# A gated-GELU block in two-level Winograd form: unit 4 in an order of its own, its sums on GpSimd, and operands of the down stage asked for sooner

## The chip, the cores and the metric

The kernel runs on one core of a Trainium2 chip. A core has TensorE (PE in the profile, with its weight loads as PEld), VectorE (DVE), ScalarE (ACT), GpSimd (POOL) and SyncE (SP, here the queue that issues all transfers), an on-chip memory in 128 partitions (SBUF), eight accumulation banks (PSUM) and 16 DMA engines. The metric is the device time of one execution in microseconds; three executions before the change took 537.00, 539.53 and 540.08 us, median 539.53.

## The reference

```python
B, S, Dm, Df = 1, 2048, 1024, 3584          # bfloat16 inputs
g = jnp.einsum("bsd,df->bsf", x, w_gate)
u = jnp.einsum("bsd,df->bsf", x, w_up)
h = jax.nn.gelu(g, approximate=True) * u
return jnp.einsum("bsf,fd->bsd", h, w_down)
```

## The kernel before

**Passes and units.** The 2048 tokens are two passes `p` of 1024, each cut into two halves `c` of 512 (a bank holds 128 x 512 numbers). The 3584 hidden columns are 14 units `u` of 256. Gate and up of a unit are computed as a 2 x 2 block product (contraction halves, column halves, token halves) with seven products in place of eight, Winograd's form. The weight side needs sums `s1` to `s4` (four-chunk tiles of 128 x 512, for gate and up each), the token side differences `t1` to `t4` and a cast `tb`. A product of four chunks is four matmuls of 128 x 128 x 512.

**Units 0 to 3** run one pass at a time (`items`, `unit`). At the end of the last item GpSimd also makes what unit 4 needs.

**Units 4 to 13** (`JOINT = 4`) run both passes together, and three of the seven products are cut once more by the same form. `X` is s4 times tb, `H` is s3 times t3, `K` is the raw quarter times t4. Each becomes seven half products `X1` to `X7` of two matmuls (14 in place of 16). They need new sums: `split_b` or `split_b3` make `n1`, `n2`, `n4` and an in-place difference from the token side, once for all units; `split_sums` (through `half_sums`) makes four half-size tiles `q1` to `q4` from the weight side, in every unit. `H` is cut from unit `DIVIDED7` on; before that it runs whole (16 matmuls).

**What sets the order.** The order is written out by hand. `SEQUENCE` is a list of steps of one joint unit; each step is issued to its engine at its place, and every engine works through its own list in order. `P1pi`, `P6pi`, `P5pi`, `S`, `G`, `X`, `H`, `K` are matmuls; `p`, `u2`, `v`, `xz`, `kz`, `ky`, `y`, `f0`, `f1`, `e00`, `e10`, `e01`, `ha`, `ga`, `gb`, `hb`, `sg`, `sh` are ACT copies, casts and gelus; `c11a`, `x00`, `m11a` and their like are DVE additions and multiplications. A step with `-` belongs to the unit before. A step with `@` is a place for side work (`side_work`): sums on GpSimd for this and the next unit, loads, and the sums of the down weights. Four banks `E` and four banks `F` change places from unit to unit.

**Down weights.** The down product uses the same form with 14 chunks `j`. For each chunk, `fetch_wd` loads two tiles, `keep_whole` makes three difference tiles `m` on GpSimd, and `store_made` writes them to DRAM (`td`); `KEEPS` says in which unit. Chunks in `STAY` keep two of them in SBUF for the first down pass, the others are loaded back (`load12`).

**Down.** `down(0)` and `down(1)` follow: the raw products `e` (14 steps of four matmuls), the next 14 into `c`, then the products of sums. A step list (`agenda`, `tails`, `more_0`) places loads and DVE sums. The hidden tiles `h` are stored to DRAM (`hd`) by the units and loaded back by `load_h`. Their SBUF space holds token sums until the units no longer read them: `room` gives `tb` and three `n` the tile `h00`, `t2` and `t1` the tile `h10`, and so on. So a load of `h00` waits for the last `X` of unit 13.

**Slots.** Nearly every small tile is one of 59 slots of 2 KB per partition; a new tile waits until the last reader of the old one is done.

Of the kernel before, what the change touches and what calls it, by code (L numbers as in the profile page):

```python
# [10 lines left out]
def kernel(  # L11
# [33 lines left out]
    NU = NFB // 2  # L45
    NWARM = 7
    JOINT = 4
    DIVIDED7 = 5
    STAY = 4, 5, 6
    KEEPS = [(u, n) for u in range(5, 14) for n in range({7: 2, 9: 2, 11: 2, 13: 3}.get(u, 1))]  # L50
    H, Q, R2 = NJ // 2, N // 2, range(2)
    SLOTS = 59
    SEAM = 3
    LAG = 3
    BIG12 = (0, 2), (8, 10)
    AT12 = [0, 0, 2, 2, 5, 5, 9, 12, 16, 18, 22, 27, 29, 31], [4, 4, 8, 8, 12, 12, 15, 16, 18, 20, 22, 27, 29, 31]
    AT12S = [6, 7, 9, 10, 13, 14, 16, 18, 20, 28, 29, 30, 31, 33]
    EARLY = 8
    AT73 = [30 + 2 * j if j < 7 else 38 + j for j in range(NJ)]
# [32 lines left out]
    def pool(out, a, b, op):  # L92
        nc.gpsimd.tensor_tensor(out=out, in0=a, in1=b, op=op)  # L93
# [200 lines left out]
                got.append(t)  # L294
        return n

    def split_b3(part, eng=pool):
        n = ns.setdefault("t3", [[], [], [], []])
        for k in range(2):
            b11, b12, b21, b22 = [T[p]["t3"][h + k] for h in (0, 2) for p in range(2)]  # L300
            if part == k:
                n1, n2, n4 = [slot([P, N], f32r, "n") for _ in range(3)]
                eng(n1, b12, b11, SUB)
                eng(n2, b22, n1, SUB)
                eng(n4, b21, n2, SUB)
                for i, t in ((0, n1), (1, n2), (3, n4)):
                    n[i].append(t)
            if part == 2:
                eng(b12, b22, b12, SUB)
                n[2].append(b12)  # L310

    def half(ps, lhs, rhs, fresh=False):
# [1 line left out]
            matmul(ps, lhs[:, k], rhs[k], fresh and k == 0, k == 1)  # L314

    SEQUENCE = (
        "@start -a00u P100 -a10u P101 @tb.0 -a00z P111 -m22a p101 @tb.1 -a01u P110 p100 -v11+ "
        "-g21a P601 -a01z @keep p110 P600 -a11u -hb2 X1 u201 -m21a P610 u200 -m22b xz1 X5 -a10y "
        "P501 p111 -a10z @s3 u210 X6 -a11z @store P500 v01 -a11y xz6 S0 -g21b x6y X7 @t3.0 v00 "
        "-m21b P510 sg c11a xz7 X2 X4 v10 @t3.1 P611 x00 f0 x01 ha H1 @t4.0 X3 u211 x7y S1 ga x10 "  # L320
        "@s1 H5 e00 m12a P511 @free gb c11b y5 H6 m11a H2 v11 K1 @t4.1 e10 x11 G0 kz1 v00+ H7 f1 "
        "H3 m12b K6 @late e01 @s2 e11 G1 ha2 e10y kz6 H4 K5 v10+ sh K2 hb v01+ @s4 K7 ky5 K3 m11b "
        "K4 kz7 @end "
    ).split()

    def joint_ops(u, E, F):
# [137 lines left out]
    def keep_whole(j):  # L464
        ra, rb = wraw.pop(j)
        m = made[j] = [slot([P, N], f32r, "m") for _ in range(3)]
        pool(m[0], ra[:, N:], ra[:, :N], SUB)
        pool(m[1], rb[:, N:], m[0], SUB)
        pool(m[2], rb[:, :N], m[1], SUB)

    def store_made(j):
        if j in STAY:
            q12[j] = made[j][:2]
        for n, m in enumerate(made.pop(j)):
            nc.sync.dma_start(out=td[:, j, n], in_=m.bitcast(f32))

# [116 lines left out]
        at_tail(1, -1 if n < 11 else 2 * n - 20, fetch12, n)  # L593
    for j in range(NJ):
        for last in range(2):
            at_tail(last, AT12[last][j], lambda j, last=last: load12(j, BIG12[last]), j)
        at_tail(0, 49 + 0.65 * j, load4, j)
        at_tail(0, 54 + 0.55 * j, make_sa, j)
    for t in range(H):
# [295 lines left out]
    def at_p5(n):  # L895
        u, p = items[n]
        if n == 0:
            pool_behind(t["t4"][-1])
            new_s(2, "s1", "s2", "s3", "s4")
        elif n == 1:  # L900
            new_s(3, "s1", "s2", "s3", "s4")
        elif n == 2:
            T[1] = sums_t(1, pool, place1)
            T[1].make("t1", "t2", "t3", "t4")
        elif n == 3:
            new_s(0, "s1", "s2", "s3", "s4")
            ss.pop(2), ss.pop(3)
            new_s(2, "s1", "s2")
        elif n == 4:
            new_s(2, "s3", "s4", "sa")  # L910
            new_s(3, "s1", "s2")
        elif n == 5:
            new_s(3, "s3", "s4", "sa")
            new_s(JOINT, "s1", "s2")
        elif n == 6:
            new_s(JOINT, "s4")

    keeps = {}
    for j, (u, n) in zip([*range(4), *range(7, NJ), *STAY], KEEPS):
        keeps[u, n] = j  # L920

    def load_next(u):
# [11 lines left out]
    def side_work(u, what):  # L934
        def made(kind, n):
            if (u, n) in keeps:
                kind(keeps[u, n])

        more = u + 1 < NU
        name, part = what[:2], int(what[3:]) if what[2:3] == "." else None  # L940
        if what == "start":
            if u == JOINT:
                load_next(u + 1)
            made(fetch_wd, 1)
        elif what == "keep":
            made(keep_whole, 0)
            if u == JOINT:
                split_b3(0, dve)
                split_b3(1)
                ns["t4"] = split_b("t4", dve, place_n)  # L950
        elif what == "store":
            made(store_made, 0)
            made(fetch_wd, 2)
        elif what == "s3":
            new_s(u, "s3")
            if u == JOINT + 1:
                split_b3(2)
        elif name == "tb":
            if u > JOINT:
                half_sums(u, name, part)  # L960
        elif name == "t3":
            half_sums(u, "t4" if u == JOINT else name, part)
            if more and part == 1:
                made(keep_whole, 1)
        elif what == "t4.0" and not more:
            half_sums(u, name, 0)
            half_sums(u, name, 1)
        elif what == "t4.1" and not more:
            made(keep_whole, 1)
            made(keep_whole, 2)  # L970
        elif name == "t4" and u > JOINT:
            half_sums(u, name, part)
        elif name in ("s1", "s2", "s4"):
            if more:
                new_s(u + 1, what)
        elif what == "late":
            made(store_made, 1)
            if (u + 1, 0) in keeps:
                fetch_wd(keeps[u + 1, 0])
        elif what == "end":  # L980
            made(store_made, 2)
            load_next(u + 2)
        if not more:
            last_loads(what)
# [2 lines left out]
    loads = {(0, 0): [3], (1, 1): [0], (3, 0): [2], (5, 0): [JOINT]}  # L987

    def last_loads(what):
        for n in {"start": range(4), "store": range(4, 8), "t4.0": range(8, 11), "s1": range(11, NJ)}.get(what, ()):  # L990
            fetch12(n)
        if what == "free":
            new_h(0, 0)
            for j0, j1 in ((0, 2), (2, 6), (6, 10), (10, NJ)):
                load_h(0, 0, 0, j0, j1)
            new_h(1, 0)
            for j0, j1 in ((0, 4), (4, 8), (8, NJ - 2)):
                load_h(0, 1, 0, j0, j1)
        if what == "end":
            new_h(1, 1), new_h(0, 1)  # L1000
            for j0, j1 in ((0, 4), (4, 8)):
                load_h(0, 0, 1, j0, j1)
                load_h(0, 1, 1, j0, j1)
                load12(j0 // 2, BIG12[0])

    with tc.manual_schedule(engines={ENG.Activation}):
        for n, (u, p) in enumerate(items):
# [41 lines left out]
            def p4(c12):  # L1049
                times(p, 2 * u, 1, gelu(c12[0]), c12[1])  # L1050
                if first:
                    whole_p4(u, p, odd, ss[u], after_first, behind_p4)
                else:
                    if n == len(items) - 1:
                        more_room()
                        ns["tb"] = split_b("tb", pool, place_n)
                        half_sums(JOINT, "tb", 0), half_sums(JOINT, "tb", 1)
                    whole_p4(u, p, (Ea, Eb)[b], ss[u], ahead_of_p4, behind_p4)

            if first:  # L1060
                banks = odd, cc, dd
# [9 lines left out]
        last = None  # L1071
        for u in range(JOINT, NU):
            now = joint_ops(u, E, F)
            for name in SEQUENCE:
                if name[0] == "@":
                    side_work(u, name[1:])
                elif name[0] != "-":
                    now[name]()
                elif last:
                    last[name]()  # L1080
            last = now
            E, F = F, E
# [4 lines left out]
    def more_0(step):  # L1087
        if step == 0:
            load_h(0, 0, 1, 8, NJ)
            load_h(0, 1, 1, 8, NJ - 1)  # L1090
        if step in (56, 59, 61):
            kh, c = {56: (0, 0), 59: (1, 0), 61: (0, 1)}[step]
            new_h(kh, c)
            for j0, j1 in ((0, 4), (4, 8), (8, NJ)):
                load_h(1, kh, c, j0, j1)
        if step == 46:
            fetch_early(0), fetch_early(4)
        if step == 63:
            new_h(1, 1)
            for j0, j1 in ((0, 4), (4, 8), (8, NJ)):  # L1100
                load_h(1, 1, 1, j0, j1)
# [33 lines left out]
```

## Time and profile before

| what | value |
|---|---|
| three runs | 537.00, 539.53, 540.08 us |
| profiled execution, its own time | 536.89 us |
| its span on the chip | 535.1 us |
| mean granted TensorE clock | 0.997 |
| PE busy | 523.2 us (98%) |
| DVE, ACT, POOL busy | 398.1, 290.9, 338.0 us |
| first matmul of unit 4, of the first down pass | 108.8 us, 356.9 us |
| last matmul ends | 531.8 us |

The units and the two down passes follow each other, so the span is read by stages. The page gives each engine's busy time in 40 slices and by group of instructions; a matmul counts as busy from its start to a modelled end (about 0.4 us), while matmuls follow each other every 0.22 to 0.23 us, so gaps are read from starts. The trace lacks some matmul records: a lone step of 0.42 to 0.46 us between two starts is one missing record.

### The profile page before, as it was taken

Reading aid. Unit: us, or ns where it says so; the run is one execution under the profiler, and the core shown is the slowest. Engines: PE = TensorE matmul, PEld = TensorE weight load, DVE = VectorE, ACT = ScalarE, POOL = GpSimd, SP = SyncE. Lnnn points to the kernel's source line nnn. Section 1 sums busy time; section 2 is a strip of 40 time slices with the busy share of each in tenths; the row PEclk is TensorE's granted clock in tenths of the full one; section 3 lists DMA queues with packets and bytes.
Section 4 is the critical chain, followed back from the end, with each engine's and each line's share of the span. In section 5 each row is a group of like instructions: output and inputs, shape, how many; then the busy total and the mean of one; then the engine's idle time right before and its main releaser. Section 6 shows DMA issues by size and latency. Waiting matters only on the chain.

```text
span 535.1 us, 7968 instructions
## 1 busy us (share of the span) xinstructions
PE 523.2 (98%) x2362; PEld 369.9 (69%) x2393; DVE 398.1 (74%) x597; ACT 290.9 (54%) x533; POOL 338.0 (63%) x344
## 2 busy tenths in 40 slices
PE   9999999997999999999999999989999999999997
PEld 5568686865676766767666776754688885488887
DVE  2984646599779898898979888894889335868934
ACT  3545655554687867878786877852125501132430
POOL 1169999999999989999999999940000000000394
PEclk9999999998999999999999999999999999999999
DMA  9687641330526274554727273899987999993642
GB/s 245 140 205 154 133 119 50 108 108 21 165 101 217 79 226 153 164 157 154 255 78 253 85 240 121 291 331 405 400 301 215 389 367 384 392 319 113 220 129 69
DMA packets 106538, 107.75 MB, mean 201 GB/s; under 512 B 19712, under 2 KB 84864, under 8 KB 106496
## 3 DMA queue, kind: packets, MB, share of 16 engines
q1 hardware_dynamic: 106496, 107.25, 62.6%
q8 instruction: 19, 0.31, 0.3%
q14 instruction: 23, 0.19, 0.1%
HBM read 74.58 MB, written 29.49 MB: 194 GB/s over the span
## 4 chain that ended last, share of the span: by engine, by line
PE 90%; SPq 4%; DVE 3%; DMA 2%; issue 1%; ACT 0%; DVEq 0%; ACTq 0%
PE bank L111 90%; SPq L779 2%; DVE h L90 2%; DMA h<-hd 1%; DVE n L90 1%; SPq L785 1%; DMA x<-in_x_dram 0%; SPq L132 0%; DVE w L90 0%; SPq L765 0%; DVE st L90 0%; DVE p L90 0%; DVE xz L90 0%; ACT bank L335 0%; ACT p L344 0%
## 5 line engine op out<-in xcount | busy, mean ns | idle before, releaser
L111 PE MATMUL bank<-h,s 128*128 128x512 f32 x472 | 129.6, 401 | 4.6 <-ACT u L107 3.5
L93 POOL TENSOR_TENSOR q<-q 128x256 fp32r<-128x256 f32 x28 | 24.3, 900 | 149.7 <-PE bank L111 149.2
L111 PE MATMUL bank<-xT,w 128*128 128x512 bf16 (+1 forms) x448 | 107.8, 376 | 1.3
L111 PEld LDWEIGHTS bank<-h,s 128*128 128x128 f32 x472 | 88.8, 188 | 26.4 <-ACT u L107 4.0
L93 POOL TENSOR_TENSOR s<-w 128x512 fp32r<-128x512 bf16 (+1 forms) x82 | 87.2, 1084 | 13.1 <-DMA w<-in_w_gate_dram 11.7
L111 PEld LDWEIGHTS <-w 128*128 128x128 bf16 x504 | 45.0, 98 | 59.4 <-issue 14.1
L111 PE MATMUL bank<-t,s 128*128 128x512 f32 x276 | 74.6, 402 | 0.0
L107 ACT COPY p<-bank 128x512 f32<-128x512 f32 x76 | 42.7, 590 | 34.7 <-PE bank L111 29.1
L111 PE MATMUL bank<-q 128*128 128x512 f32 x248 | 61.5, 390 | 0.0
L111 PEld LDWEIGHTS bank<-t,s 128*128 128x128 f32 x276 | 52.4, 190 | 12.1
L90 DVE TENSOR_TENSOR q<-h,h 128x512 fp32r<-128x512 bf16 x56 | 38.3, 685 | 21.3 <-DMA h<-hd 21.3
L111 PEld LDWEIGHTS bank<-q 128*128 128x128 f32 x248 | 46.5, 188 | 9.8
L107 ACT COPY u<-bank 128x512 f32<-128x512 f32 x62 | 35.9, 592 | 24.5 <-PE bank L111 23.2
L93 POOL TENSOR_TENSOR s<-s,s 128x256 fp32r<-128x256 f32 x57 | 43.3, 786 | 1.9 <-PE bank L111 0.2
L93 POOL TENSOR_TENSOR s<-s,w 128x512 fp32r<-128x512 f32 (+1 forms) x40 | 41.2, 1047 | 1.7 <-PE bank L111 0.5
L93 POOL TENSOR_TENSOR s<-w,s 128x512 fp32r<-128x512 bf16 (+1 forms) x40 | 41.5, 1054 | 0.0
L111 PEld LDWEIGHTS <-h 128*128 128x128 bf16 x224 | 21.7, 98 | 28.3 <-DMA h<-hd 2.3
L90 DVE TENSOR_TENSOR xz<-bank,xz 128x512 f32<-128x512 f32 x40 | 27.5, 690 | 15.9 <-PE bank L111 7.4
L111 PE MATMUL bank<-raw,h 128*128 128x512 bf16 x156 | 34.7, 379 | 1.6 <-DMA h<-hd 1.4
L93 POOL TENSOR_TENSOR m<-raw,m 128x512 fp32r<-128x512 bf16 x28 | 34.6, 1234 | 2.2
L102 ACT CAST tb<-raw 128x512 fp32r<-128x512 bf16 x28 | 17.0, 632 | 33.4 <-DMA raw<-in_w_down_dram 14.6
L90 DVE TENSOR_TENSOR h<-g,bank 128x512 bf16<-128x512 f32 x42 | 28.6, 684 | 6.4 <-ACT g L205 3.5
(125 smaller groups left out, 929.8 us busy)
## 6 DMA issues: line engine op xcount, KB each, us to landing
raw<-in_w_down_dram SPq DMA_DIRECT2D x72, 256.0 KB, 4.0
q<-td SPq DMA_DIRECT2D x62, 256.0 KB, 5.3
hd<-h SPq DMA_DIRECT2D x109, 128.0 KB, 1.8
td<-m SPq DMA_DIRECT2D x42, 256.0 KB, 2.5
h<-hd SPq DMA_DIRECT2D x18, 512.0 KB, 7.4
w<-in_w_gate_dram SPq DMA_DIRECT2D x8, 512.0 KB, 4.4
w<-in_w_up_dram SPq DMA_DIRECT2D x8, 512.0 KB, 5.5
w<-td SPq DMA_DIRECT2D x4, 1024.0 KB, 8.7
```

What stands on the lines that cost most here:

```text
L90: nc.vector.tensor_tensor(out=out, in0=a, in1=b, op=op)
L93: nc.gpsimd.tensor_tensor(out=out, in0=a, in1=b, op=op)
L102: nc.scalar.copy(out=t, in_=src)
L107: nc.scalar.copy(out=t, in_=ps)
L111: nc.tensor.matmul(ps, lhsT=lhs, rhs=rhs, start=start, stop=stop, skip_group_check=True)
L779: nc.sync.dma_start_transpose(out=XT[p, c][ko], in_=x2[r0 : r0 + N, ko * P : (ko + 1) * P])
L785: got = queue.dma_start(out=wf[:, i, k0:k1], in_=src[k0 * P : k1 * P, 0 : 2 * P].rearrange("(ko ki) f -> ki ko f", ki=P),)
```

## The change

Unit 4 gets a list of its own, `SEQUENCE_FIRST`; the other units get a new `SEQUENCE`. The eight sums that split `t4` go from DVE inside unit 4 to GpSimd, issued after the sums for `tb` at the end of the last item. The three-and-three sums and two differences that split `t3` go from unit 4 and 5 (the first three on DVE) to units 5 and 6, all on GpSimd; `H` is cut from unit 6 instead of 5, and `s3` of unit 4 is made before its `s4`. Sums of down weights start with unit 7 instead of 5; the last two chunks are loaded, summed and stored inside the first down pass. The chunks that stay in SBUF are 9 to 13 instead of 4, 5 and 6. In unit 13 the first two loads of `h00` are issued at a new place `@room`, right behind the last `X` step, and `h10` at `@late`; the first four pairs of raw down chunks go to a big `w` tile.

```diff
-    DIVIDED7 = 5
-    STAY = 4, 5, 6
-    KEEPS = [(u, n) for u in range(5, 14) for n in range({7: 2, 9: 2, 11: 2, 13: 3}.get(u, 1))]
+    DIVIDED7 = 6
+    STAY = range(9, 14)
+    KEEPS = [(u, n) for u in range(7, NU) for n in range({7: 2, 9: 2, 11: 2, 13: 3}.get(u, 1))]
-    BIG12 = (0, 2), (8, 10)
-    AT12 = [0, 0, 2, 2, 5, 5, 9, ...
+    BIG12 = (0,), (8, 10)
+    AT12 = [0, 0, 1, 2, 4, 5, 9, ...
     SEQUENCE = (
...
+        "@start -m22a P110 -a10u P100 -a10y @tb.0 P101 -a10z p100 P111 -a00u -g21b @keep -v11+ S0 "
+        "-hb2 -a00z p101 P600 -a11u p110 X1 -m22b -g21a P601 u200 -a01u P610 @tb.1 xz1 c11a "
+        "@store u201 -a11z P500 f0 @s3 -a01z X6 u210 -a11y P501 v00 -m21a xz6 P510 -m21b p111 X5 "
+        "v01 @t3.0 X7 ha X2 x6y X4 xz7 P611 x00 v10 x01 sg H1 X3 @room ga @t3.1 x7y S1 u211 x10 "
+        "e00 H5 @t4.0 P511 @free c11b gb y5 m11a H6 @t4.1 H2 v11 m12a K1 e10 x11 G0 @s1 kz1 m12b "
+        "H7 f1 H3 v00+ K6 e01 @late e11 G1 hb @s2 e10y kz6 H4 v10+ K5 sh K2 ha2 v01+ K7 ky5 m11b "
+        "K3 @s4 K4 kz7 @end "
+    SEQUENCE_FIRST = (
+        "@start P101 p101 P110 p110 P100 p100 P111 p111 P601 u201 P610 u210 P600 u200 P611 u211 "
+        "P501 v01 P500 v00 X1 xz1 S0 S1 c11a c11b ha P510 v10 P511 v11 X6 xz6 f0 X2 m11a x00 X5 "
+        "x6y ga X4 X7 xz7 f1 X3 x10 x01 x7y m12a x11 gb G0 G1 m12b hb @t4.0 @t4.1 H2 sg sh K1 kz1 "
+        "m11b @s1 H3 v00+ H4 @late @s2 v01+ v10+ K6 kz6 K5 ky5 ha2 K2 K4 K7 kz7 K3 @s4 @end "
+    ).split()
...
         elif n == 6:
-            new_s(JOINT, "s4")
+            new_s(JOINT, "s3", "s4")
...
         elif what == "keep":
             made(keep_whole, 0)
-            if u == JOINT:
-                split_b3(0, dve)
-                split_b3(1)
-                ns["t4"] = split_b("t4", dve, place_n)
...
         elif what == "s3":
-            new_s(u, "s3")
-            if u == JOINT + 1:
+            if u == DIVIDED7:
+                split_b3(1)
                 split_b3(2)
+            if u > JOINT:
+                new_s(u, "s3")
...
-        elif name == "t4" and u > JOINT:
+        elif name == "t4":
             half_sums(u, name, part)
+            if u == JOINT + 1 and part == 1:
+                split_b3(0)
...
+        if what == "room":
+            new_h(0, 0)
+            for j0, j1 in ((0, 2), (2, 6)):
+                load_h(0, 0, 0, j0, j1)
...
+                    if n == len(items) - 1:
+                        ns["t4"] = split_b("t4", pool, place_n)
...
-            for name in SEQUENCE:
+            steps = SEQUENCE_FIRST if u == JOINT else SEQUENCE
+            for name in steps:
...
+        if step in (18, 20):
+            fetch_wd(NJ - 2 + (step == 20))
+        if step in (24, 28):
+            keep_whole(NJ - 2 + (step == 28))
+        if step in (32, 36, 40):
+            store_made(NJ - 3 + (step - 32) // 4)
```

## The prediction

> **What bounds the kernel now.** First the page's busy times, then the list of waits over all engines.
>
> ```profile
> PE 523.2 (98%) x2362; PEld 369.9 (69%) x2393; DVE 398.1 (74%) x597; ACT 290.9 (54%) x533; POOL 338.0 (63%) x344
> ...
> ACT bank L335 <- DVE p L90: 4.4, 1, 4.4
> ...
> PE bank L111 <- ACT u L107: 3.5, 1, 3.5
> ...
> PE bank L111 <- DMA h<-hd: 1.4, 2, 1.1
> ...
> PE bank L111 <- POOL s L93: 1.0, 1, 1.0
> ```
>
> TensorE is the bound. It waits in three places only (its first 0.8 us aside), and time is won there or by fewer matmuls. The timeline shows the first two, in unit 4 (start, duration, engine; in brackets the idle time before and what ended it):
>
> ```profile
> 109.70 1.28 DVE L90 TENSOR_TENSOR n<-h,t 128x512 fp32r<-128x512 f32 x1
> 113.78 1.74 POOL L93 TENSOR_TENSOR w<-tb,w 128x512 fp32r<-128x512 f32 x1
> 116.70 0.50 PE L111 MATMUL bank<-h,s 128*128 128x512 f32 x1 [1.03 <-POOL s L93]
> 123.96 1.76 DVE L90 TENSOR_TENSOR h<-t,h 128x512 fp32r<-128x512 f32 x1
> 124.11 1.04 PE L111 MATMUL bank<-xT,w 128*128 128x512 bf16 x3
> 127.00 0.59 ACT L335 COPY bank<-p 128x512 f32<-128x512 f32 x1 [4.39 <-DVE p L90]
> 128.06 0.56 ACT L107 COPY u<-bank 128x512 f32<-128x512 f32 x1
> 128.68 1.84 PE L111 MATMUL bank<-h,s 128*128 128x512 f32 x4 [3.53 <-ACT u L107]
> ```
>
> DVE works from 109.70 to 125.7 on eleven token sums. Behind them stands `c11a`; the ACT seed `f0` waits for it, the copy `u2` stands behind that seed, and PE waits for the copy. GpSimd shares the delay: a token sum takes it 1.28 to 1.30 us at 104 to 110 us and 1.60 to 1.74 us while DVE adds from SBUF too.
>
> The windows around the long wait give the clock (columns: PE, PEld, DVE, ACT, POOL busy, granted clock, DMA share, GB/s):
>
> ```profile
> 124.00:128.60 4.60, 1.10 (x5) 0.31 (x4) 4.57 (x7) 1.60 (x4) 4.52 (x5) 1.00 0.01 2
> 128.60:132.60 4.00, 3.92 (x10) 2.97 (x10) 3.68 (x7) 1.78 (x4) 4.00 (x5) 0.57 0.18 61
> 132.60:136.00 3.40, 3.40 (x16) 2.13 (x16) 1.64 (x3) 2.51 (x6) 3.40 (x4) 1.00 0.33 101
> ```
>
> After it the matmuls start 0.43 us apart until 132.4. The third place is the change to the down stage:
>
> ```profile
> 351.66 4.58 SPq L608 DMA_DIRECT2D h<-hd  x7
> ...
> 355.12 0.61 PE L111 MATMUL bank<-h,sh 128*128 128x512 f32 x2
> 356.86 1.04 PE L111 MATMUL bank<-raw,h 128*128 128x512 bf16 x4 [1.12 <-DMA h<-hd]
> 358.19 1.04 PE L111 MATMUL bank<-raw,h 128*128 128x512 bf16 x4 [0.29 <-DMA h<-hd]
> ```
>
> The first loads of `h00` are issued 4 us ahead of use and land 5.2 and 6.5 us after issue.
>
> The chain of waits has two runs of PE a divided unit, from 166.03 to 189.97: 23.94 us for 106 matmuls, 0.226 us each. The starts of the matmuls then give the losses. Unit 4: 115.28 to 116.70, 1.19 us over one step; 124.77 to 128.68, 3.68 over; nine steps from 128.68 to 132.43 take 3.75 in place of 2.03, 1.72 over. Sum 6.59. At the down stage: 355.34 to 356.86 and 357.51 to 358.19, 1.29 + 0.45 = 1.74. More than 8.3 us can't be won by ending waits.
>
> **The change part by part.**
>
> *Eleven sums leave DVE in unit 4.* 109.7 to 125.7 is freed. What DVE has left there takes one operand from a bank and 0.60 us from start to start, some fifteen steps. So `c11a` follows `S0`, and nothing of the old chain is late. Gain 6.59, if GpSimd keeps up.
>
> *GpSimd gets eight of them between `tb` and unit 4's half sums.* Its ledger, without a pause since before 99 us: `s3` and `s4` of unit 4 from 101.76, two pairs at 2.25: 106.27. Eight `tb` sums at 1.285 (four take 5.14 from 104.02): 116.55. Four half-size sums, 2.90 as at 149.50 to 152.40: 119.45. Eight `t4` sums at 1.285: 129.73. First two `t4` half sums 1.45: 131.2, the others 132.4. Then for unit 5 `s1` 134.65, `s2` 136.9, first `s4` 138.0, second 139.15, first `tb` half sums 140.6.
>
> PE's ledger, from 108.84 at 0.226: `X6`, the first to need a `tb` sum, stands behind 58 matmuls: 121.9, its sum is there at 118.1. `K6` needs the second `t4` half sum and stands behind 96: 130.5 against 131.2. So **PE waits 0.7 us at `K6`**. `K7` and `K3` find theirs. Unit 4 (108 matmuls) ends at 133.9. In unit 5 `P600` (behind 20) wants `s2` at 138.5, 1.6 us after it is made; `X1` (24) at 139.4, 1.4 us after; `X6` (38) at 142.5, 1.9 after. Two of the products `h<-v,v` with both operands in SBUF lengthen a GpSimd step by up to 0.45 each (1.62 at 145.41 against 1.17); 0.5 us is left then. The bounds of the cost at `K6`: 0 if a sum takes 1.25; if each `t4` sum takes the 1.69 of 110 to 115 us, 8 x 0.4 = 3.2 more, 3.9 in all. I take 0.7, since those slow rows all lie beside DVE sums from SBUF, and unit 4 has none left.
>
> *Unit 5 runs `H` whole.* 16 matmuls for 14: +0.45 us. Its copies and seeds for `H` go; ACT (18.7 of 24 us busy) wasn't waited for, so nothing.
>
> *`t3` sums move to units 5 and 6; down sums leave units 5 and 6.* Unit 5 gives up three down sums (1.16 + 2.74), two differences (2.55) and four half sums (2.9), and gets three sums (3.9); unit 6 gives up three down sums (1.61 + 2.45) and gets five steps of 1.28. Going on, `s3` of unit 6 is made at 169.2; `H1` behind 60 matmuls from 158.3 wants it at 171.9. 2.7 us in hand; without it each late microsecond is one of PE. Nothing.
>
> *The new order in units 5 to 13.* PE has no wait in these units before, so the order can't gain. The narrow places, counted in matmuls: `H1` rewrites the bank that `xz7` copies, 8 matmuls (1.81) behind `X7`; result 0.2 and copy 0.6 leave 1.0. `S0`, now behind 16 matmuls (3.6), rewrites the bank that `a10z` reads; from `H4`, ten matmuls before the unit's end (2.26), run `v01+`, `m11b`, `m22a`, `a10u`, `a10y`, `a10z`: 5 x 0.60 + 1.15 and 0.2 for the result, 4.4 of 5.9. `K4` and `f1` have about 1.0. Nothing; upper end in the rivals.
>
> *`h00` asked for at `@room`.* The last `X` of unit 13 ends 42 matmuls, 9.5 us, before the down stage in place of the 4 us. With 5.2 and 6.5 us to landing both are there. On SP ahead of them stand only stores of `m21a` and `m21b`, finished earlier in the unit, and raw loads. `h10` moves back behind three `td` stores that wait for GpSimd, which had its first late sums of unit 13 done 1.7 to 5.4 us before the units' end; `h10` is used 12.6 us into the stage. Gain 1.74; bounds 0 (they land as late as now) and 1.74.
>
> *Last two down chunks in the first down pass.* Two times three sums (3.6 us each) on a GpSimd that is idle from 354 on; four loads and nine stores of 256 KB that SP issues in 0.4 to 0.5 us each (six stores ran there before), four chunk loads fewer (five chunks stay, not three), three issues more for chunks 2 and 3. Sums of chunk 12 are asked for at step 24 and used at step 40, 16 steps of 0.90: 14 us for 4. The DMA engines are busy 0.97 of 356 to 446, yet PE has no gap there; net traffic is some 0.75 MB more, 2 us at 400 GB/s. Nothing; if the cover went, a late chunk would cost up to the 5.3 us of such a load.
>
> **Sum.** -6.59 + 0.45 + 0.7 - 1.74 = -7.2 us: 536.9 becomes 529.7 on the profiled execution. That one is 2.6 below the median of the three runs, near their lowest (537.0). From the median 532.3. I take **531.8**, a little under that, as one run in three was at the low level. What a measurement here tells from no change is about 0.5%, 2.7 us.
>
> **The rivals.**
>
> *A. GpSimd late in unit 4.* For it: it is 98% busy there, and the 1.60 to 1.74 rows. Against: those lie beside SBUF additions of DVE. With 1.69 a sum PE waits 3.9 us, as long as the 3.68 that halved the clock: 1.72 more. Gain 7.2 - 3.2 - 1.7 = 2.3: 537.2. The trace brackets the point where a wait costs the clock too: 1.3 us didn't, 3.7 did. In "TensorE: Matmul & The Clock Gate", section "What's actually happening", the Trainium skill puts it at an idle window of about 3.4 us that runs freely; by that a wait of 3 us pays no 1.72, by the trace alone it may, and the time at that length would be 534.6 by the one and 536.3 by the other. Against this rival, the Trainium skill's "SBUF — State Buffer", section "Who interferes with whom", says that a DVE step with one SBUF input leaves GpSimd alone; the trace agrees (1.28 to 1.30 beside such steps).
>
> *B. The down stage waits as before.* The DMA share from 333 to 356 is 0.89, and loads asked sooner may queue behind the weights. Against: 9.5 us against 6.5. 1.74 back: 533.5.
>
> *C. Slower: `S0` waits for DVE in every unit from 5 on.* DVE is busy 21 of 24 us, and the list puts four of its steps before `S0`. If DVE is 2.7 us behind its steps at a unit's start, 1.2 us are lost nine times, 10.8: 543.1. It turns the result slower from 0.8 us a unit on (DVE 2.3 behind). Against: 1.4 us in hand by the count above, and DVE's sum of steps a unit is 20.3 us.
>
> *D. No change:* a wait of 4.5 to 8.7 us that the rows don't show, in the down stage's transfers say: 536.8 to 541.
>
> **How the numbers follow.** Forecast 0.59, B 0.12, A 0.12, C 0.08, D 0.09. The forecast's own range, 0 to 1.5 us at `K6` and the spread of the runs, is 529 to 534, and holds B's time. With A's 537.2 the cases hold 0.83, less some tails: 528.5 to 538. Faster by over 0.5% (below 536.8): forecast, B and half of A, 0.77. Slower (over 542.2): C and a little of A and D, 0.13. The rest 0.10.
>
> **What would show it.** Right: no PE wait over 1.5 us from 109 to 134, clock 1.00 there; a short one at `K6` on GpSimd at about 130.5; unit 5 starting at 133 to 134; no wait for `h<-hd` at the first down matmul, which comes near 350; PE spacing 0.226 in all units. Wrong: GpSimd `t4` sums of 1.6 us, a wait in each unit at the first `S` step, or a gap inside the first down pass.

## The result and the profile after

| | before | after |
|---|---|---|
| executions | 537.00, 539.53, 539.91, 540.08 us | 531.27, 532.30, 532.64, 533.18 us |
| median | 539.72 us | 532.47 us |
| profiled execution, its span | 536.89, 535.1 us | 531.27, 529.5 us |
| mean granted clock | 0.997 | 0.999 |

The ratio is 0.9874 with a 95% interval of 0.9837 to 0.9911: 4.8 to 8.8 us are gained, 6.8 in the middle.

The page's busy times and the timeline of the changed kernel around `K6` and at the change to the down stage (start, duration, engine; in brackets the idle time before and what ended it):

```profile
PE 522.4 (99%) x2364; PEld 369.4 (70%) x2395; DVE 388.0 (73%) x584; ACT 288.3 (54%) x529; POOL 347.2 (66%) x351
...
127.92 1.29 POOL L93 TENSOR_TENSOR h<-t,h 128x512 fp32r<-128x512 f32 x1
129.92 0.68 POOL L93 TENSOR_TENSOR s<-s,w 128x256 fp32r<-128x256 f32 x1
130.65 0.30 PEld L111 LDWEIGHTS bank<-h,s 128*128 128x128 f32 x2 [0.57 <-POOL s L93]
...
340.72 0.80 SPq L616 DMA_DIRECT2D h<-hd  x2
350.19 0.61 PE L111 MATMUL bank<-h,sh 128*128 128x512 f32 x2
```

The eighth `t4` sum takes 1.29 us, the half sum that `K6` needs ends at 130.6, and PE's next weight load comes at once behind it: a matmul starts 0.53 us after the one before it in place of 0.23, so 0.30 us are lost. That is the only wait of PE in unit 4. `h00` is asked for at 340.72, and the first down matmul follows at 350.64 without a wait.

Where the time went can be told by stages, from the starts of the matmuls in both traces (unit lengths from first raw matmul to first raw matmul; where the trace lacks the record of unit 4's first matmul, that one is put one step of 0.23 us behind the matmul ahead of it; 23.9 us is a divided unit without waits, 87.7 a first down pass without waits):

| stage | before | after | difference | predicted |
|---|---|---|---|---|
| unit 4 | 31.09 | 24.78 | -6.31 | -6.59 + 0.7 |
| unit 5 (`H` whole) | 23.93 | 24.35 | +0.42 | +0.45 |
| units 6 to 13 | 191.71 | 192.78 | +1.07 | 0 |
| wait at the first down matmul | 1.29 | 0 | -1.29 | -1.29 |
| first down pass | 88.17 | 88.75 | +0.58 | -0.45 |
| second down pass | 86.51 | 86.51 | 0 | 0 |

With 0.1 us less ahead of unit 4 this is the 5.6 us between the two spans; the prediction had 7.2. Between the medians there are 7.25 us. The interval holds both, so the executions can't tell which is nearer.

Some stages differ between executions of the same code, and the traces of the experiments below show by how much. Where the code is that of the changed kernel, unit 4 takes 24.78 to 25.00 us (six traces), unit 7 24.55 to 25.55 (eight), unit 13 24.65 to 25.21 (seven) and the first down pass 87.68 to 89.27 (eight). In the traces of the kernel before and of its two variants, unit 7 takes 24.18 to 24.86 and unit 13, without the wait at the down stage, 23.93 each time. So the gain in unit 4 and a loss in unit 13 are clear of that spread. The loss in unit 7 is not, and the size of the +0.58 in the first down pass holds for one execution only.

### The profile page after: what moved, and what is told of

The parts are those of the page before. It is cut to its first block, busy times and chain, and to the rows that moved or that the text cites. A ratio compares the mean times of both kernels' runs of the same rounds, so it can differ in the third digit from the quotient of the medians.

```text
span 529.5 us, 7937 instructions
## 1 busy us (share of the span) xinstructions
PE 522.4 (99%) x2364; PEld 369.4 (70%) x2395; DVE 388.0 (73%) x584; ACT 288.3 (54%) x529; POOL 347.2 (66%) x351
## 5 line engine op out<-in xcount | busy, mean ns | idle before, releaser
L111 PE MATMUL bank<-xT,w 128*128 128x512 bf16 (+1 forms) x448 | 106.0, 376 | 1.4
L93 POOL TENSOR_TENSOR q<-q 128x256 fp32r<-128x256 f32 x28 | 25.6, 946 | 106.6 <-DMA q<-td 106.0
L93 POOL TENSOR_TENSOR s<-w 128x512 fp32r<-128x512 bf16 (+1 forms) x82 | 85.1, 1055 | 13.7 <-DMA w<-in_w_gate_dram 12.6
L111 PE MATMUL bank<-t,s 128*128 128x512 f32 x280 | 76.7, 400 | 0.3 <-ACT u L107 0.3
L93 POOL TENSOR_TENSOR s<-w,s 128x512 fp32r<-128x512 bf16 (+1 forms) x40 | 44.9, 1140 | 0.0
L93 POOL TENSOR_TENSOR s<-s,s 128x256 fp32r<-128x256 f32 x54 | 38.7, 740 | 1.4
L93 POOL TENSOR_TENSOR m<-raw 128x512 fp32r<-128x512 bf16 x14 | 16.8, 1199 | 33.0 <-DMA raw<-in_w_down_dram 33.0
L93 POOL TENSOR_TENSOR m<-raw,m 128x512 fp32r<-128x512 bf16 x28 | 35.9, 1282 | 2.2
```

Of the source, the lines that this page charges most:

```text
L111: nc.tensor.matmul(ps, lhsT=lhs, rhs=rhs, start=start, stop=stop, skip_group_check=True)
```

## The experiments

Each run has its time as a ratio to the kernel before on the same chip, and the difference to the changed kernel is that of the ratios times 538 us. Those differences are uncertain by some 2 us, so the verdicts rest mainly on the lengths of the stages in the trace, with the spreads above in mind.

### Unit 4: the order, the engine, or the number of sums

**`t4_on_dve`**: the eight `t4` sums go back to DVE, the order stays.

```diff
-                        ns["t4"] = split_b("t4", pool, place_n)
+                        ns["t4"] = split_b("t4", dve, place_n)
```

> The changed kernel with the eight t4 token sums of unit 4 back on DVE, its order of unit 4 kept. Theory, by positions: DVE adds from 109 to about 121.5 us at 1.2 to 1.8 us a sum, c11a follows by 122, the seed f0 is first needed by G0 behind 70 matmuls (124.7 us), so PE has no long wait; the t4 half sums are early, so the 0.3 us at K6 goes; GpSimd's tb sums take 1.6 us beside DVE. Time -0.3 to +0.8 us to the changed kernel: the order of unit 4 is what carries the gain. Rival, as the prediction put it (eleven sums on DVE are the cause of the stall): a wait of 3 us or more and half clock behind it, +5 us.

Ratio 0.9865 (0.9818 to 0.9912), the time of the changed kernel. Unit 4 takes 24.86 us, 0.1 more than in the changed kernel. The DVE rows of its timeline:

```profile
112.38 1.78 DVE L90 TENSOR_TENSOR h<-h,h 128x512 fp32r<-128x512 f32 x1
114.08 1.78 DVE L90 TENSOR_TENSOR h<-t,h 128x512 fp32r<-128x512 f32 x1
...
120.32 1.23 DVE L90 TENSOR_TENSOR h<-t,h 128x512 fp32r<-128x512 f32 x1
121.47 0.68 DVE L90 TENSOR_TENSOR p<-bank,p 128x512 f32<-128x512 f32 x1
```

DVE adds at up to 1.78 us a sum beside GpSimd, as in the kernel before, and still `c11a` (121.47) comes early enough: PE loses 0.45 us, at `X7`. So, with the new order of unit 4, it was not needed to take these eight sums from DVE.

**`one_order` and `one_order_t4_dve`**: unit 4 in the order of the other units, with the sums on GpSimd and with the `t4` sums on DVE.

```diff
-            steps = SEQUENCE_FIRST if u == JOINT else SEQUENCE
+            steps = SEQUENCE
```

> The changed kernel with unit 4 in the same order as units 5 to 13, the sums still on GpSimd. Theory: X6 stands behind 38 matmuls (117.4 us) and its half sum is made at 118.0, K6 behind 84 (128.4 with that) and its half sum is made at 130.6: waits of 0.6 and 2.2 us in place of 0.3, no fall of the clock, +2.5 us (1.5 to 3.2) to the changed kernel. Rival (only the engine of the sums matters): no waits, +0.

> Both of the two edits: unit 4 in the order of the other units, and its t4 sums on DVE. Theory: c11a, asked for behind 34 matmuls (116.5 us), waits for DVE till 122; f0 and the copy u210 stand behind it on ACT, and P510 (118.8 us) waits for that copy till about 124, 4.9 us, then half clock for some 4 us, 1.7 more: +6 us (4.5 to 7.5) to the changed kernel, nearly all that the change had won in unit 4. If each edit alone costs little and both together this much, neither the order nor the engine alone is the cause. Rival (the two add up): the sum of the two runs beside it.

Ratios 0.9931 (0.9909 to 0.9953) and 0.9975 (0.9950 to 1.0001), 3.1 and 5.4 us over the changed kernel. Unit 4 takes 29.07 and 29.09 us, 4.3 more in both. The timelines show the long waits, first of `one_order`, then of `one_order_t4_dve`:

```profile
130.39 0.73 PE L111 MATMUL bank<-h,s 128*128 128x512 f32 x2 [2.27 <-POOL s L93]
131.66 2.17 PE L111 MATMUL bank<-t,s 128*128 128x512 f32 x4
```

```profile
116.97 1.75 POOL L93 TENSOR_TENSOR w<-tb,w 128x512 fp32r<-128x512 f32 x1
120.03 0.80 PE L111 MATMUL bank<-h,s 128*128 128x512 f32 x1 [3.14 <-POOL s L93]
121.05 1.91 PE L111 MATMUL bank<-t,s 128*128 128x512 f32 x4
```

The waits in `one_order` came at the places expected (`X6` 0.43, `K6` 2.43 from start to start), but the clock fell behind the second, which was not expected: four matmuls take 2.17 us. In `one_order_t4_dve` the size was right and the cause was not: PE waits at `X6` for GpSimd, whose `tb` sums take 1.6 to 1.75 us beside DVE, before it comes to the copy that stands behind `c11a`.

**`before_first_order`**: the other way round, the kernel before with unit 4's new order. That list has no place `@keep`, so the sums that stood there are issued at `@start`, and `s3` is made one step sooner.

```diff
-            for name in SEQUENCE:
+            for name in SEQUENCE_FIRST if u == JOINT else SEQUENCE:
...
         if what == "start":
             if u == JOINT:
                 load_next(u + 1)
+                split_b3(0, dve)
+                split_b3(1)
+                ns["t4"] = split_b("t4", dve, place_n)
...
-            new_s(JOINT, "s4")
+            new_s(JOINT, "s3", "s4")
```

> The kernel before with only unit 4's order taken over from the changed kernel: its eleven DVE sums of unit 4 stay on DVE, three t3 sums on GpSimd, h00 and the down chunks as before; s3 of unit 4 is made one step sooner, since that order has no place for it. Theory (the order carries unit 4's gain, since it asks for DVE's first answer late): DVE adds from 109.7 to 125.7, c11a follows at 126.3, f0 at 126.9; G0 behind 70 matmuls (124.7) waits 2.3 us and may halve the clock for 3 to 4 us: unit 4 takes 27 to 28.5 us in place of 30.9, -2.5 to -4 us to the kernel before. Rival, the prediction's words (the sums on DVE are the cause, whatever the order): unit 4 stays at 30 us or more, 0 to -1 us.

Ratio 1.0009 (0.9987 to 1.0030): nothing is gained. Unit 4 takes 30.26 us. DVE, ACT and PE in its timeline:

```profile
125.35 0.68 DVE L90 TENSOR_TENSOR p<-bank,p 128x512 f32<-128x512 f32 x1
126.06 0.63 ACT L351 ACTIVATE p<-p 128x512 f32<-128x512 f32 x1 [6.70 <-DVE p L90]
127.53 0.60 ACT L107 COPY xz<-bank 128x512 f32<-128x512 f32 x1
128.28 2.05 PE L111 MATMUL bank<-h,s 128*128 128x512 f32 x4 [4.19 <-ACT xz L107]
```

The first wait was expected at `G0`, behind `f0`. But the gelu `ha` stands ahead of the copies `v10`, `v11` and `xz6` on ACT, it needs `c11a`, and `X7` needs `xz6`: PE is held at matmul 66 already, for 4.35 us, and the clock falls. My theory that the order alone carries the gain is refuted.

The six kernels together, with the sums that DVE makes in unit 4:

| kernel | DVE sums | order of unit 4 | unit 4, us |
|---|---|---|---|
| before | 11 | of the other units (old) | 31.09 |
| `before_first_order` | 11 | its own | 30.26 |
| `one_order_t4_dve` | 8 | of the other units (new) | 29.09 |
| `one_order` | 0 | of the other units (new) | 29.07 |
| `t4_on_dve` | 8 | its own | 24.86 |
| after | 0 | its own | 24.78 |

The whole gain needs two things at once: the own order, and fewer than eleven sums ahead of `c11a`. Eight are few enough; nine and ten were not run. Three sums more put `c11a` from 121.5 to 125.4 and cost 5.4 us (these two kernels differ on GpSimd too, which has three `t3` sums in unit 4 of `before_first_order`, and behind unit 4). The step from eight to none is worth 0.1, less than traces of the same code differ.

### How near GpSimd is to the path at `K6`

**`gp_1_more` and `gp_2_more`**: the last `t4` sum is made twice or three times; the result is the same.

```diff
-            eng(n4, b21, n2, SUB)
+            for _ in range(1 + k * again):
+                eng(n4, b21, n2, SUB)
```

> The changed kernel with one more GpSimd sum of 128x512 ahead of unit 4's t4 half sums (the last t4 sum made twice). Theory (K6 is the narrow place, GpSimd has nothing in hand there): one sum is 1.29 us, PE waits 1.6 us at K6 in place of 0.3, granted clock stays 1.00 (1.2 us of wait left it alone in the kernel before): +1.3 us to the changed kernel. Rival (GpSimd has slack and the 0.3 is something else): +0.3 or less.

> The same with two more sums. Theory: a wait of 2.9 us at K6, and since 2.3 us of idle time halved the clock in the run with unit 4 in the order of the others, half clock for 3 to 4 us behind it: +2.6 for the wait and 1.3 to 1.8 for the clock, +4 us. Rival, by the Trainium skill's rule of an idle window of about 3.4 us (TensorE: Matmul & The Clock Gate, What's actually happening): clock stays 1.00 and +2.6 us.

Ratios 0.9906 (0.9889 to 0.9924) and 0.9971 (0.9946 to 0.9996), 1.7 and 5.2 us over the changed kernel. Unit 4 takes 26.28 and 28.88 us, 1.5 and 4.1 more. The windows of `gp_2_more` around the wait (from:to, length, then busy time and count of PE, PEld, DVE, ACT and POOL, granted clock, DMA share, GB/s):

```profile
120.00:134.82 14.82, 11.82 (x51) 8.55 (x51) 8.80 (x14) 7.55 (x15) 14.43 (x15) 0.99 0.11 37
134.82:138.23 3.41, 3.41 (x10) 2.06 (x9) 2.07 (x2) 1.44 (x3) 3.41 (x4) 0.53 0.75 205
138.23:145.00 6.77, 6.72 (x31) 4.20 (x31) 6.70 (x12) 4.64 (x9) 6.61 (x9) 1.00 0.34 92
```

One sum late is 1.5 us of PE, with the clock at 1.00 throughout. Two are 2.8 us of wait and 1.3 of clock inside unit 4: the record of half clock runs from 134.60 to 138.01, and it begins 1.4 us after PE has resumed (133.24). (The windows are cut 0.2 us later, hence 0.53.) So GpSimd has nothing in hand at `K6`. Rival A of the prediction had the `t4` sums 3.2 us late and counted 1.7 for the clock: here a delay of 2.8 us cost the clock in the profiled execution, and a delay of 1.5 did not. The profiled execution of `gp_2_more` is the slowest of its eight, and it lost 4.3 us in the second down pass as well, where the edit changes nothing; the last section comes back to that.

### The change to the down stage

**`h00_at_free`**: the changed kernel with the first loads of `h00` back at `@free`.

```diff
-            new_h(0, 0)
-            for j0, j1 in ((0, 2), (2, 6)):
-                load_h(0, 0, 0, j0, j1)
+            pass
         if what == "free":
-            for j0, j1 in ((6, 10), (10, NJ)):
+            new_h(0, 0)
+            for j0, j1 in ((0, 2), (2, 6), (6, 10), (10, NJ)):
```

> The changed kernel with the first two loads of h00 put back at @free. Theory (the loads were late, asking sooner won 1.74 us): PE waits again for h00 at the first down matmul and once more for the second part, 1.3 to 2.0 us together, and the time is 1.7 us over that of the changed kernel. Rival (the transfers would have been there in the new order of unit 13 anyway, since @free stands 32 matmuls ahead of the down stage): no wait, time as the changed kernel.

Ratio 0.9904 (0.9870 to 0.9937), 1.6 us over the changed kernel: the size expected, but the interval also holds the changed kernel's 0.9874, and the loss in the trace comes from another place. SP and PE in its timeline:

```profile
339.28 5.42 SPq L535 DMA_DIRECT2D raw<-in_w_down_dram  x3
344.79 1.84 SPq L616 DMA_DIRECT2D h<-hd  x4
...
351.32 6.87 PE L111 MATMUL bank<-w,h 128*128 128x512 bf16 x31
...
395.85 1.17 PE L111 MATMUL bank<-m,q 128*128 128x512 f32 x4 [1.69 <-DVE q L90]
```

PE waits for nothing at the first down matmul: the loads are issued 6.5 us ahead of it even at `@free`. The profiled execution, the slowest of seven, loses its time later, in a first down pass of 91.75 us in place of 88.75; the section on that pass shows where.

**`before_room`**: the kernel before with the sooner loads alone.

```diff
-... H1 @t4.0 X3 u211 ...
+... H1 @t4.0 X3 @room u211 ...
+        if what == "room":
+            new_h(0, 0)
+            for j0, j1 in ((0, 2), (2, 6)):
+                load_h(0, 0, 0, j0, j1)
         if what == "free":
-            new_h(0, 0)
-            for j0, j1 in ((0, 2), (2, 6), (6, 10), (10, NJ)):
+            for j0, j1 in ((6, 10), (10, NJ)):
```

> The kernel before with only the first two loads of h00 asked for sooner, at a new step behind X3, three raw loads of chunks (those of s1) no longer ahead of them. Theory (h00 was late because SP stood in raw loads that waited for slots): issued some 3 us sooner, the 1.3 us at the first down matmul goes and the 0.45 behind it too, -1.3 to -1.8 us. Rival (the run with h00 back at @free had no wait there either, and lost in the first down pass): the later loads come late in their stead, 0.

Ratio 0.9973 (0.9960 to 0.9987): 1.45 us won, as expected, and both waits are gone (first pass 87.68 us). SP in the kernel before, and then in this run:

```profile
344.36 6.74 SPq L528 DMA_DIRECT2D raw<-in_w_down_dram  x6
351.19 0.42 SPq L214 DMA_DIRECT2D hd<-h  x1
351.66 4.58 SPq L608 DMA_DIRECT2D h<-hd  x7
```

```profile
346.66 4.54 SPq L528 DMA_DIRECT2D raw<-in_w_down_dram  x3
351.30 1.08 SPq L608 DMA_DIRECT2D h<-hd  x2
352.45 1.44 SPq L528 DMA_DIRECT2D raw<-in_w_down_dram  x3
```

Six raw loads stood ahead of `h00` in the kernel before, in a queue that works in order; here three of them come after it, and the lead of 6.6 us over the down matmul (357.86) is enough. In `h00_at_free` three stood ahead as well, since `@s1` comes behind `@free` in the new order, and the lead was the same 6.5 us. So in the changed kernel `@room` was not needed for the start of the down stage; the new order of the loads had already ended that wait.

### The first down pass and the down chunks

**`chunks_early`** and, with other units for the double chunks, **`chunks_keeps`**.

```diff
-        if step in (18, 20):
-            fetch_wd(NJ - 2 + (step == 20))
-        if step in (24, 28):
-            keep_whole(NJ - 2 + (step == 28))
+        if step in (0, 1):
+            fetch_wd(NJ - 2 + (step == 1))
+        if step in (8, 12):
+            keep_whole(NJ - 2 + (step == 12))
```

```diff
-... range({7: 2, 9: 2, 11: 2, 13: 3}.get(u, 1)) ...
+... range({8: 2, 10: 2, 12: 2, 13: 3}.get(u, 1)) ...
```

> The changed kernel with the loads of down chunks 12 and 13 issued at steps 0 and 1 of the first down pass in place of 18 and 20, and their sums on GpSimd at steps 8 and 12 in place of 24 and 28. Theory (the 0.6 us wait at 396.66 is DVE late: its raw loads queued behind these four loads on SP, then four DVE sums at 1.5 to 1.65 us in place of 0.69 beside the GpSimd sums): DVE's sums from 385 on take 0.69, no wait of PE in the first down pass, -0.8 us (-0.3 to -1.2) to the changed kernel. Rival (the DMA engines, busy 0.92 to 0.99 there, are the limit): the wait stays, somewhere in the pass.

> The same, and the units that make two down chunks are 8, 10, 12 in place of 7, 9, 11. Theory: in unit 7 ACT's copy xz1 waits 1.3 us for a slot that the second chunk's sums free late, since GpSimd comes late out of unit 6 with its t3 sums; with one chunk in unit 7 that PE wait of 0.4 goes and none takes its place: -0.4 us more, -1.2 in all to the changed kernel. Rival (the wait moves to unit 8): as the run beside it.

First the changed kernel in the pass, GpSimd and DVE, and PE behind them:

```profile
386.67 1.62 POOL L93 TENSOR_TENSOR m<-raw 128x512 fp32r<-128x512 bf16 x1
387.18 1.65 DVE L90 TENSOR_TENSOR q<-h,q 128x512 fp32r<-128x512 bf16 x1
391.92 0.68 DVE L90 TENSOR_TENSOR q<-h,h 128x512 fp32r<-128x512 bf16 x1
396.66 4.82 PE L111 MATMUL bank<-m,q 128*128 128x512 f32 x20 [0.61 <-DVE q L90]
```

Four DVE sums take 1.49 to 1.66 us while GpSimd sums the last chunks, and 0.68 as soon as GpSimd is done. `chunks_early` has the GpSimd sums at 374.57 to 383.6, where DVE is not needed soon; its sums from 384.27 on take 0.69, and the pass takes 88.00 us without a PE wait over 0.25 us. In the time nothing shows: 0.9873 (0.9854 to 0.9891).

That the two engines slow each other here is shown. That the slow sums alone cost PE its time is not: the same four slow sums stand in every trace with this code of the pass, also where PE doesn't wait. What differs is when they begin. The first of them needs a raw load, which SP issued at 379.81, behind the four chunk loads at 377.06:

```profile
385.73 1.53 DVE L90 TENSOR_TENSOR q<-raw 128x512 fp32r<-128x512 bf16 x1 [7.16 <-DMA raw<-in_w_down_dram]
```

| trace | first slow sum, us into the pass | first down pass, us |
|---|---|---|
| `old_order` | 33.05 | 87.68 |
| `one_order` | 34.25 | 87.71 |
| `dve_3_more` | 34.59 | 88.23 |
| `gp_1_more` | 34.69 | 88.27 |
| `one_order_t4_dve` | 34.74 | 88.38 |
| `gp_2_more` | 35.02 | 88.68 |
| after | 35.08 | 88.75 |
| `t4_on_dve` | 35.64 | 89.27 |
| `h00_at_free` | 38.11 | 91.75 |

From about 34.1 us on, each microsecond that this load comes later is one of PE (in `one_order` the first of the four sums took only 1.21, which made up for its start). `chunks_early` takes away both causes, the loads ahead on SP and the slow neighbour, so it doesn't separate them, and its gain of 0.75 us lies within this spread. `chunks_keeps` is slower, 0.9920 (0.9902 to 0.9939): the wait left unit 7 (23.90 us) and came back in units 8, 10 and 12 (24.58 to 24.69 each), unit 13 took 25.25, and the first down pass 89.43. The wait moved and multiplied.

### Units 5 to 13: DVE's room, and the order

**`dve_3_more`**: three DVE steps more ahead of `a10y` in each unit, written to a spare tile that nobody reads. **`old_order`**: the step list of the kernel before for units 5 to 13, with `@room` put behind `X3`.

```diff
-        plus("-a10y", E[1][0], "ky5")
+        def thrice():
+            for _ in range(3):
+                dve(spare, E[1][0], t["ky5"], ADD)
+            dve(E[1][0], E[1][0], t["ky5"], ADD)
+        ops["-a10y"] = thrice
```

> The changed kernel with three more DVE steps of 0.60 us (a bank and an SBUF operand, result unused) ahead of a10y in units 5 to 13. Theory (S0 waits for a10z; the trace leaves 1.15 us between them): 1.8 - 1.15 = 0.65 us a unit, nine times, +5.9 us; a wait at S0 in each of these units. Rival (DVE, busy 21 of 24 us, catches up elsewhere and PE never waits): +0. Other rival (several banks are late behind it): +1.8 us a unit, +16.

> The changed kernel with units 5 to 13 in the order of the kernel before (with the step that asks for h00 behind X3), unit 4 as changed. Theory (the 0.67 us lost in unit 7 and the 0.96 in unit 13 come with the new order): units 5 to 13 as in the kernel before, -1.6 us to the changed kernel. Rival (they come from GpSimd's new load in units 6 and 7, and the order is indifferent): the same time, waits in unit 7 again.

`dve_3_more`: 1.0097 (1.0074 to 1.0119), 12 us over the changed kernel, twice what I expected. DVE and PE in unit 8:

```profile
208.87 1.32 DVE L90 TENSOR_TENSOR h<-v,v 128x512 bf16<-128x512 f32 x1
210.90 2.14 DVE L90 TENSOR_TENSOR spare<-bank,ky 128x512 bf16<-128x512 f32 x3
213.69 0.69 DVE L90 TENSOR_TENSOR kz<-bank,kz 128x512 f32<-128x512 f32 x1
214.43 1.02 PE L111 MATMUL bank<-xT,w 128*128 128x512 bf16 x4 [1.29 <-DVE kz L90]
```

The wait is at `S0` as priced, but the steps stand 0.72 us apart in place of 0.60, so `a10y` comes 2.1 us later and not 1.8. And there was less in hand than expected: in unit 8 of the changed kernel `a10z` ends at 209.32 and `S0` starts at 209.77, 0.45 us later. The nine units lose 0.4 to 2.1 us each, 1.3 on average.

`old_order`: 0.9875 (0.9849 to 0.9901), the time of the changed kernel. Unit 7 loses 1.06 us before one matmul; in the new order its largest wait was 0.42 to 1.43 us in eight traces. The timeline gives ACT's reason:

```profile
190.90 0.59 ACT L107 COPY xz<-bank 128x512 f32<-128x512 f32 x1 [2.35 <-POOL m L93]
```

So the wait in unit 7 doesn't come from the order: ACT's copies wait for a free slot. What frees the slot last differs between the traces. Here it is a chunk sum on GpSimd, and so in the changed kernel (1.28 us). In three more runs ACT waits for such a sum and then for the store of a hidden tile, `hd<-h`; in four others (`t4_on_dve`, `one_order`, `one_order_t4_dve`, `gp_2_more`) for such a store alone, 2.3 to 3.1 us. The kernel before waits in unit 7 for such a store as well, 1.68 us in its trace and 2.35 in `before_room`. `chunks_keeps` shows that a second down chunk in the unit is part of the cause; that GpSimd is late because of its `t3` sums in unit 6 is argued, and no run shows it. Unit 13 took 24.32 us with the old order, against 24.65 to 25.21 in the seven traces with the new one and 23.93 in the kernel before. So a part of that loss seems to belong to the new order, though the old one has a single trace.

## Why the prediction was right, and where it was not

**The size in unit 4 was right** (-5.89 predicted, -6.31 measured), and so was the chain that it took away. The ledger of GpSimd held within 0.6 us: `t4` sums 1.27 to 1.30, half sum ready at 130.6 for 131.2. `K6` cost 0.30 in place of 0.7.

**The cause in unit 4 was told wrongly.** The step "eleven sums leave DVE in unit 4 ... gain 6.59" credits the engine. The runs show that eight of the eleven could have stayed (24.86 against 24.78 us), and that without the own order the leaving of these eight is worth nothing (29.07 with them on GpSimd, 29.09 on DVE). Two conditions have to hold. GpSimd's answers have to be asked for late: `X6` stands behind 58 matmuls in the own order and 36 or 38 in the others, `K6` behind 96 and 84. PE waits at `X6` in both `one_order` runs, and at `K6` too in the one that has the `t4` sums on GpSimd. And DVE has to be done before `X7` (66 matmuls, about 124 us) wants the copy behind `c11a`: with the three `t3` sums gone it is done at 121.5, with them at 125.4. The prediction had both in hand, the positions and DVE's rows; it used the positions only to see whether GpSimd would keep up.

**`H` whole in unit 5** cost 0.42 for 0.45. **The change to the down stage** won 1.74 as predicted, but the step "`h00` asked for at `@room`" names only one of two sufficient causes; the loads had queued behind raw loads on SP, and the new places of those raw loads ended that too.

**Two terms set to nothing were not nothing.** Units 6 to 13 lost 1.07 us in the profiled execution: unit 7 took 24.56 for 24.18, unit 13 24.89 for 23.93, and the others 0.04 less each. The prediction checked the matmuls' own operands in these units (`H1` of unit 6 above all), and not the slots that ACT's copies need; for unit 7, where the kernel before waits too, the ranges of the two kernels overlap. The first down pass lost 1.03 us beside the 0.45 it won. "14 us for 4" counted GpSimd's time for chunk 12. It left out DVE, which works from SBUF beside it, though the same prediction had quoted such rows for unit 4, and it left out that DVE's raw loads now stand on SP behind the chunk loads. By the table above this loss was 0 to 1.6 us in other traces. With `K6` (0.4 better) these are the 1.6 us by which the sum 529.7 missed the profiled 531.27.

**That the medians lie 7.25 us apart, next to the sum of 7.2, is partly luck.** The profiled executions show 5.6. The executions of the kernel before differ with their clock: in one round of nineteen the two at a mean of 0.999 and 1.000 took 535.9 and 535.1 us, the eleven at 0.996 and 0.997 536.9 to 539.0, the six at 0.994 538.3 to 539.4. The profiled one, at 0.997, has one stretch of half clock; those at 0.994 would have two, like the trace of `before_room` with its 6.83 us of half clock and the same mean (an estimate from the means). The four executions of the changed kernel are at 0.999 and 1.000. So part of the difference between the medians comes from stretches that the profiled execution didn't have, and that the prediction didn't count. The forecast of 531.8 was set a little under the 532.3 that the sum gave from the median, and lies 0.7 under the measured 532.47.

**Rival C** (`S0` waits for DVE) didn't come, but its room was smaller than the 1.4 us that were counted: three steps that held DVE up by 2.1 us cost 1.3 us a unit, which leaves about 0.7.

## What to carry to other kernels

When an engine's early work holds up a step that others stand behind, there are two repairs: less work ahead of it, or a later first use; find out from the positions in the list which is needed before moving work to another engine. A term set to nothing because one engine has time must be checked for the neighbours as well: what runs beside it from the same memory, which buffers its last step frees, and which loads queue behind its loads. In a queue that works in order, a load is late because of what stands ahead of it, so look there before asking for it sooner. And before a stage of one trace is explained, compare the same stage in other traces of the same code: here one of them varied by 1.6 us.

## What the runs showed of the hardware

**The clock falls in stretches of one length.** The trace's records of the granted clock show 0.5 for 3.41 us in the kernel before and in four of the runs, and for 6.83 us, twice that, in `before_room`. Within a trace the stretches lie on a fixed grid: in `gp_2_more` they begin at 134.60 and 527.13 us, 115 times 3.413 apart, and in the kernel before at 128.98 and, behind its last matmul, 535.16, 119 times. So where one begins does not follow the wait: 0.6 us before PE resumed in `one_order_t4_dve`, 0.3 us after it in the kernel before, 1.4 us after it in `one_order` and `gp_2_more`. Single waits of up to 2.02 us (from start to start, less one step; `before_first_order` at the down stage) left the clock alone, those of 2.4 us and more in the profiled executions halved it. The Trainium skill, "TensorE: Matmul & The Clock Gate", section "What's actually happening", has a free-running window of 3413 ns, and these stretches agree with it. It also asks for an idle window of about 3.4 us; here much less was enough. If the windows are counted back from the fall, PE was idle for 2.05 of 3.41 us in the window before it, in both `one_order` and `gp_2_more` (an estimate from those records). Nor need it be one wait: ahead of the second stretch of `gp_2_more`, in its second down pass, five matmuls in a row (524.14 to 526.88) each wait for a GpSimd sum `q`, 0.55 to 0.69 us apart where such matmuls of 256 columns else follow each other every 0.12. With a window that runs freely, the same wait need not cost the clock each time, which fits the spread of the executions: those of `gp_2_more` have mean clocks from 0.992 to 0.999 and times from 533.66 to 540.55 us, those of `gp_1_more` times from 532.53 to 534.03.

**GpSimd and DVE slow each other, both ways.** In the first down pass DVE sums with all operands in SBUF went from 0.68 to between 1.49 and 1.66 us beside GpSimd sums, and those from 1.16 to 1.62. In unit 4 of `t4_on_dve` it was up to 1.78 for DVE and 1.75 for GpSimd, whose sums there take 1.26 to 1.30 in the changed kernel. The Trainium skill, "SBUF — State Buffer", section "Who interferes with whom", says that a DVE step with two SBUF inputs contends with a GpSimd step that reads SBUF; these rows agree, and the DVE steps with one operand in a bank kept their 0.68 to 0.70 us in unit 4.
